# Sharing the fourth pairs' rows in three steps of two transfers, with a new order of all engines' work, in a fused attention, gMLP and channel-mix kernel

## The chip, the core and the metric

The kernel runs on one core of one Trainium2 chip. The core has TensorE (PE, with its weight loads PEld), VectorE (DVE), ScalarE (ACT), GpSimd (POOL) and SyncE (SP), each with a program of its own that it works off in order. They wait for one another by semaphores; transfers run on 16 DMA engines. The metric is the device time of one execution in microseconds (us).

## What is computed

Three blocks stand behind one another. Only `x` passes between them.

```python
# attention: B=2, H=8, S=768, D=48
for t in range(S):
    cur = einsum('bhd,bhe->bhde', u * k[t], v[t])
    y[t] = einsum('bhd,bhde->bhe', r[t], state + cur)
    state = w[t][..., None] * state + einsum('bhd,bhe->bhde', k[t], v[t])
x = y.transpose(0, 2, 1, 3).reshape(B, S, 384)
# gated MLP: d_ff = 1024, halves u and v of 512
h = gelu(x @ w_in)
v_n = layernorm(v) * g_ln
x = x + (u * (w_sg @ v_n + b_sg)) @ w_out
# channel mix
xk = mu_k * x + (1 - mu_k) * x_prev
xr = mu_r * x + (1 - mu_r) * x_prev
out = sigmoid(xr @ w_r) * (relu(xk @ w_k) ** 2 @ w_v)
```

Matrices of weights come in float64; the kernel rebuilds float32 values from their two halves.

## The kernel before

**Tiling.** Tokens are cut into four groups g = 2b + half of 384 (batch b, half of the sequence), each in three chunks of 128. The attention is computed by chunks: within one through a masked 128 by 128 matrix, between them through a state. Heads go in pairs: per group there are four *units* (unit i is pair i % 4 of group i // 4, 16 in all). Per group three *packs* of 128 rows hold the decay products. A pack's rows are 48 + 16 + 48 + 16: two heads of a pair, and in each 16-row strip a third of the fourth pair. So the fourth unit of a group (3, 7, 11, 15) reads its k and r from a gathered tile `six`, filled from the three packs by token `6` (L284 to L287), and its result must be spread again over 16-row strips of xT: that is `share` (L409 to L412).

**Order.** All instructions are laid down by a table of tokens, ORDER (L34 to L88), read from left to right; one token is one step, which may issue on any engine. Within an engine the table's order is the program's order. No scheduler changes it. The tokens that matter here, with the unit's or the pack's number behind the letter:

- per pack: `L`, `q` load the decays wt and the rows rk; `D` a scan (L258); `a`, `j`, `g` the bound, reciprocal and backward scan (L261, L265, L268); `K` and `d` products with rk (L276, L272); `6` as above.
- per unit: `V` loads vT (L301, a tile with one buffer), `w` loads vk (L305, two buffers); on PE `T` (ptr, L325), `A` (pA, L336), `P` (pa, L340), `S` (pkv, L348), `I` (py, L392), `J` (py, L398); on DVE `m` am (L366), `n` t = pa * vT (L372, the last reader of vT), `s` the state scan sc (L377), `O` the result py + t (L407); on ACT `k`, `p`, `c`, `x` copies, among them kvs (L361; a GpSimd memset of kvs is L358), wps (L353), sx (L383); `o` is `share`.
- `X` splits xT in a high and a low part (xs_hi L431, xs_lo L433); `v` is one of the generators of the first dense product, pv, of one group and chunk (L197 to L199, three products of the high and low parts), with layer statistics through GpSimd (L450 to L452: add, power, add) and ACT (L449, L454, vn_hi L459); `u` (pu), `M` (ps), `W` (po), `E` (pk), `R` (pr), `Z` (po) are the others.
- `C<i>.x` etc. are the steps that rebuild and split piece i of the weights (DVE L163, L168, L172, L178; ACT L175, L184): 0 to 11 w_in, 12 to 23 w_sg, 24 to 31 w_out, 32 to 43 w_k, 44 to 59 w_v, 60 to 65 w_r.
- `e` issues one filler product on PE, `idle`, that nobody reads.

All transfers are issued by SP, in the table's order, so a transfer whose data are not ready holds up all that follow it in SP's program.

Of the kernel before, what the change touches and what calls it, by code (L numbers as in the profile page):

```python
# [40 lines left out]
C4.x V4 s3 A4 q5 C4.b x3 L5 T4 j4 m4 C8.l p5 C6.l I3 k4 C4.t g4 C4.h S4 C4.r n4 C4.q N3 d4 f4 J3 c4 K4 A5 C4.o O3 64 s4 T5 D5 x4 63 P5 m5 k5
p6 I4 w5 a5 K5 L6 j5 C6.x J4 C5.l C8.x C6.b V6 C8.b w6 O4 e e o3 C6.t e P6 C8.t C6.h g5 C8.h S5 C8.o f5 C6.o e d5 e c5 e e e C5.x e 65 s5 T6
n6 x5 A6 C5.b V5 D6 k6 I5 X0.1.h X0.2.h m6 S6 X0.0.h J5 a6 c6 C5.t X0.0.l C5.r A7 j6 w7 n5 p7 C5.h s6 T7 C5.q V7 O5 q6 x6 P7 L7 m7 k7 C7.l I6
C6.r C5.o p8 g6 C6.q S7 J6 n7 c7 X0.1.l V8 f6 v0.0 s7 q7 w8 d6 x7 D7 T8 v0.0 O6 A8 C7.x k8 K6 v0.0 I7 a7 C7.b q8 j7 X0.2.l p9 C10.l P8 C7.t
L8 g7 C7.r J7 C7.h C7.q K7 S8 d7 f7 66 v0.2 v0.0 n8 q9 c8 O7 L11 C8.r s8 v0.0 o7 C7.o T9 x8 C10.x v0.0 P9 v0.2 m8 I8 k9 D8 v0.2 w9 A9 V9
C10.b C8.q a8 C9.l J8 K8 p10 C11.l m9 v0.1 j8 C10.t g8 C10.h v0.2 C10.o f8 S9 d8 v0.1 u0.0 L9 n9 68 v0.2 D11 v0.1 P10 67 C9.x O8 u0.0 C9.b
A10 c9 C11.x V11 C9.t T10 s9 w10 C9.h C9.r D9 u0.1 x9 C11.b k10 K9 v0.1 I9 a9 C11.t u0.1 j9 C9.o C11.h S10 g9 v0.1 J9 c10 C11.o v0.1 f9 u0.3
s10 C9.q L10 O9 C13.l p11 C10.r m10 T11 x10 C25.l P11 d9 C10.q A11 u0.3 v0.2 C11.r n11 u0.2 p12 C19.l C11.q m11 V10 C13.h w11 C25.x k11 D10 B
I10 X1.0.h X1.1.h C25.b A12 a10 X1.2.h C13.o u0.2 X1.1.l J10 C19.h X1.2.l v1.1 j10 n10 w12 m12 q10 V12 g10 C20.l S11 v1.1 O10 P12 a11 C19.o
c11 j11 v1.1 C25.t v1.2 C18.l s11 f10 g11 p13 x11 d10 T12 f11 n12 I11 K10 k12 C20.h X1.0.l S12 v1.2 C20.o P13 c12 J11 v1.2 s12 T13 v1.1 O11  # L50
69 x12 u1.3 610 v1.1 k13 v1.1 I12 p14 o11 u1.3 v1.2 v1.0 C18.h v1.2 C18.o v1.2 w13 J12 v1.0 q11 V13 A13 O12 v1.0 C12.l u1.0 w14 m13 C23.l S13
u1.0 u1.1 c13 d11 v1.0 K11 v1.0 T14 s13 611 u1.1 n13 A14 x13 v1.0 P14 m14 k14 C23.h I13 C12.h C23.o C12.o S14 C21.l V14 p15 J13 c14 A15 s14
w15 C17.l O13 T15 x14 m15 P15 C21.h k15 n14 u1.2 C21.o C14.l C17.h I14 C17.o X2.1.h u1.2 X2.1.l C24.l S15 X2.0.h V15 J14 X2.2.h X2.0.l c15
X2.2.l v2.1 C14.h O14 s15 C14.o x15 C24.x C22.l n15 v2.2 v2.1 C24.b C24.t v2.1 C24.r I15 v2.2 C28.l v2.0 C24.q v2.2 C22.h v2.1 C22.o J15
C25.r C15.l v2.0 M1.0 C26.l O15 C25.q o15 v2.0 v2.2 C15.h C15.o M1.2 M1.0 C27.l | M1.0 v2.0 C25.h C24.h C25.o C24.o C26.x C28.x C26.b u2.1
C28.b C26.t C28.t C26.h M1.2 C26.r C28.h C26.o C30.l C26.q M1.3 M1.2 u2.1 C27.x C28.o C27.b C27.t C27.h C27.r C27.o C27.q C31.l C30.x C30.b
u2.2 C28.r M1.3 C28.q C29.l C30.t M1.3 C30.h C30.o u2.3 u2.2 C31.x C31.b C31.t M0.3 u2.3 C29.x C29.b C31.h C29.t C31.o C29.h C29.r C29.o
C29.q C32.l C30.r C30.q C33.l M0.1 M0.3 C31.r M0.3 C31.q C34.l C32.x C32.b C32.t C33.x M0.0 C32.r M0.1 C32.h C35.l C32.q C33.b C32.o M0.1
C34.x C33.t C34.b C33.r C34.t C33.h C39.l M1.1 C33.q C33.o M0.0 C34.h C34.r C35.x M0.0 C34.q C40.l C34.o C35.b C35.t C39.x C35.h u2.0 C39.b
C35.r C35.o C35.q C36.l C39.t M1.1 C39.h M0.2 C40.x u2.0 M1.1 X3.1.h C40.b X3.0.h C39.o X3.2.h C40.t X3.0.l C40.h C36.x C40.o C36.b v3.0  # L60
X3.1.l v2.0 C36.t v2.2 M0.2 v2.0 C36.h v2.1 M0.2 v3.1 v3.0 v2.1 C36.r v2.2 v3.0 C37.l C36.o X3.2.l C36.q v3.2 v3.1 v3.1 v3.0 C37.x u3.1 C37.b
v3.2 C37.t C37.r u3.0 v3.2 C38.l v3.1 C37.h u3.2 v3.1 C37.o u3.0 v3.1 v3.0 u3.3 C38.x v3.2 v3.0 u3.2 C38.b v3.2 C38.t u3.3 v3.2 C38.h G0.1.h
C38.o M3.3 G0.3.h G0.1.l G0.0.h G0.3.l G0.2.h G0.0.l u3.1 G0.2.l C37.q C38.r M2.0 C38.q C41.l M3.3 C39.r M3.3 C39.q C42.l C40.r C40.q C44.l
C41.x M2.2 M2.0 C41.b M2.0 C42.x C41.t C42.b C41.r C42.t C41.h C46.l C41.q C41.o M3.0 M2.2 C42.h C42.r C44.x M2.2 C42.q C43.l C42.o C44.b
C44.t C46.x C44.h C46.b C44.o M2.1 C46.t M3.0 C46.h C46.o C43.x M3.0 C43.b C43.t C43.r W0.2 C43.h C47.l M2.1 C43.q C43.o M2.1 C44.r C44.q
C45.l M3.2 W0.2 C47.x C47.b C47.t C47.h C45.x C47.o C45.b C45.t W0.0 M3.2 C45.r C45.h C48.l M3.2 C45.q C45.o C46.r C46.q C51.l W0.1 W0.0
C47.r C47.q C50.l C48.x C48.b M3.1 W0.1 G1.2.h G1.1.h C48.t C51.x G1.0.h G1.2.l C48.h C51.b C48.r G1.1.l G1.3.h C49.l G1.0.l C48.q G1.3.l
M2.3 C51.t M3.1 C51.h C51.o M3.1 C50.x C48.o C50.b C49.x C50.t C49.b C50.h W1.0 C49.t M2.3 C49.r C49.h H0 C53.l C49.q C50.r W1.2 C50.q C52.l
# [849 lines left out]
```

## Time and profile before

| | us |
|---|---|
| median of 3 runs | 349.54 (347.97 to 351.85) |
| the profiled execution | 350.13 |
| its span | 348.3 |
| PE busy in the span | 329.8 |
| DVE busy | 257.4 |
| ACT busy | 210.0 |
| POOL busy | 45.0 |

The span is the time from the first to the last instruction of the execution that was profiled. A row of the timeline gives start, duration, engine, line and operation; in brackets stands how long the engine sat idle before it, and whose end released it ("issue" where the profile names nothing). A tile's buffer number is left out of its name. DMA rows of SP (SPq) give the time of the issue, not of the transfer.

### The profile page before, as it was taken

To read this page: it belongs to the slowest core of one execution; us is meant where nothing else is said; L and a number is where in the kernel's file an instruction comes from. 1 tells how busy PE (TensorE), PEld (TensorE's weight loads), DVE (VectorE), ACT (ScalarE), POOL (GpSimd) and SP (SyncE) were. 2 spreads that over 40 slices of the span, in tenths; PEclk is the share of its full clock that TensorE was granted. 3 is DMA by queue.
4 is the path that set the end of the run, shared out by engine and by line. 5 is a ranking of instruction groups with operands and counts; after the bars stand their busy time and mean duration, and the time that the engine had idled before them with its cause. 6 is when DMAs were issued, how large, how long until landed. Compare 5 with 4: busy or idle time off the path is not lost.

```text
span 348.3 us, 6211 instructions
## 1 busy us (share of the span) xinstructions
PE 329.8 (95%) x2162; PEld 295.0 (85%) x2165; DVE 257.4 (74%) x575; ACT 210.0 (60%) x575; POOL 45.0 (13%) x92
## 2 busy tenths in 40 slices
...
GB/s 211 186 197 249 177 98 202 204 187 92 212 69 147 147 95 60 85 145 45 46 85 84 85 81 11 25 45 73 110 1 70 0 2 68 0 2 23 45 41 34
DMA packets 22435, 32.52 MB, mean 93 GB/s; under 512 B 2944, under 2 KB 18816, under 8 KB 22400
## 3 DMA queue, kind: packets, MB, share of 16 engines
...
q8 instruction: 18, 0.29, 0.4%
...
## 4 chain that ended last, share of the span: by engine, by line
PE 70%; DVE 8%; DMA 4%; ACT 4%; POOL 1%; issue 1%; SPq 1%; DVEq 0%; ACTq 0%
PE po L557 11%; PE ps L197 5%; PE ps L199 5%; PE ps L198 5%; PE pk L199 5%; PE pk L198 5%; PE pk L197 5%; PE po L199 4%; PE po L197 4%; PE po L198 4%; DMA vT<-in_rkv_dram 3%; PE pr L199 2%; PE pr L197 2%; PE pr L198 2%; PE pu L197 2%; PE pu L198 2%
## 5 line engine op out<-in xcount | busy, mean ns | idle before, releaser
L197 PE MATMUL ps<-wsg,vn_hi 128*128 128x384 f32 x96 | 32.7, 340 | 0.0
L198 PE MATMUL ps<-wsg,vn_hi 128*128 128x384 f32 x96 | 32.5, 338 | 0.0
L199 PE MATMUL ps<-wsg,vn_lo 128*128 128x384 f32 x96 | 32.5, 338 | 0.0
L199 PE MATMUL pk<-xk_hi,wk_lo 128*128 128x384 f32 x96 | 32.4, 337 | 0.0
L198 PE MATMUL pk<-xk_lo,wk_hi 128*128 128x384 f32 x96 | 32.3, 336 | 0.0
L197 PE MATMUL pk<-xk_hi,wk_hi 128*128 128x384 f32 x96 | 32.3, 336 | 0.0
L536 ACT CAST kk_hi<-kr 128x384 fp32r<-128x384 f32 x32 | 16.0, 512 | 20.1 <-PE po L557 11.3
L529 ACT ACTIVATE kr<-pk 128x384 f32<-128x384 f32 x32 | 15.7, 490 | 18.9 <-PE pk L199 15.0
L531 DVE TENSOR_TENSOR kr<-kr 128x384 f32<-128x384 f32 x32 | 17.7, 556 | 12.7 <-ACT kr L529 12.2
L560 DVE TENSOR_TENSOR rr<-po,rr 128x384 f32<-128x384 f32 x12 | 6.7, 555 | 24.6 <-PE po L199 10.0
L557 PE MATMUL po<-pl_win_hi,kk_hi 128*128 128x384 f32 x81 | 23.0, 338 | 0.0
L538 DVE TENSOR_TENSOR kk_lo<-kr,kk_hi 128x384 fp32r<-128x384 f32 x32 | 17.5, 555 | 2.6 <-ACT kk_hi L536 2.1
L383 ACT COPY sx<-sc 48x144 f32<-48x144 f32 x32 | 14.5, 454 | 8.0 <-DVE sc L377 7.6
L450 POOL TENSOR_SCALAR ln<-ln 128x1 f32<-128x1 f32 x12 | 6.3, 524 | 94.1 <-ACT vj L449 94.1
L197 PEld LDWEIGHTS ps<-wsg,vn_hi 128*128 128x128 f32 x96 | 18.0, 188 | 0.5 <-DVE sg L476 0.3
L557 PE MATMUL po<-pl_win_lo,kk_hi 128*128 128x384 f32 x63 | 18.4, 338 | 0.0
L557 PE MATMUL po<-pl_win_hi,kk_lo 128*128 128x384 f32 x54 | 18.2, 337 | 0.0
L199 PEld LDWEIGHTS pk<-xk_hi,wk_lo 128*128 128x128 f32 x96 | 18.0, 188 | 0.0
L198 PEld LDWEIGHTS pk<-xk_lo,wk_hi 128*128 128x128 f32 x96 | 18.0, 188 | 0.0
L197 PEld LDWEIGHTS pk<-xk_hi,wk_hi 128*128 128x128 f32 x96 | 18.0, 188 | 0.0
L198 PEld LDWEIGHTS ps<-wsg,vn_hi 128*128 128x128 f32 x96 | 18.0, 188 | 0.0
L199 PEld LDWEIGHTS ps<-wsg,vn_lo 128*128 128x128 f32 x96 | 18.0, 188 | 0.0
...
## 6 DMA issues: line engine op xcount, KB each, us to landing
...
```

Source lines behind the costliest of these rows:

```text
L197: T.matmul(ps, lh, rh, start=(i == 0), stop=False)
L198: T.matmul(ps, lh, rl, start=False, stop=False)
L199: T.matmul(ps, ll, rh, start=False, stop=(i == n - 1))
L383: A.copy(u.sx[o:o + D, :, o:o + D], u.sc[o:o + D, :, 1:1 + NCB].rearrange("p e c -> p c e"))
L450: G.tensor_scalar_add(ln[:, 1:2], ln[:, 1:2], EPS * DH ** 3)
L529: A.activation(kr, ps, AF.Relu)
L531: V.tensor_mul(kr, kr, kr)
L536: A.copy(hi, kr)
L538: V.tensor_sub(lo, kr, hi.bitcast(F32))
L557: T.matmul(pv[g][s], l, wv[i][r], start=st, stop=(i == KF - 1 and l is ll))
L560: V.tensor_mul(rr[g][:, s, :], pv[g][s], rr[g][:, s, :])
```

## The change

`share` becomes three steps: each call issues the two transfers of one 128-row block j. The table has `o3.0`, `o3.1`, `o3.2` where it had `o3`, and the same for 7, 11 and 15, at places of their own. The whole table is in another order, with 37 instead of 35 tokens `e`. A tile mask2 is made in step `Q` by two small GpSimd copies. Branches for `u.i < HALVES` in `scores`, `weigh` and `inner` and a step `rest` (token `h`) are new, but HALVES is 0 and no token `h` stands in the table, so they never run. All other work is the same. Line numbers move by 2 to 28: vT's load is L303, n L391, s L396, O L433, share L437 and L438.

```diff
-ORDER = """L0 q0 e Q e L1 e q1 e V0 e C0.l e D0 w0 e e a0 p0 e j0 K0 e g0 e e e e d0 f0 e e e e L2 D1 e A0 60 T0 a1 p1 m0 P0 k0 j1 K1 g1 P1 n0 f1 e d1
+ORDER = """L0 q0 e e Q e L1 e C0.l e q1 e D0 V0 e w0 e a0 p0 e w1 j0 K0 e g0 e e e e d0 f0 e e e e L2 D1 e A0 60 C0.x T0 p1 a1 m0 P0 k0 j1 C0.b g1 e e e
...
+HALVES = 0
...
+    mask2 = keep.tile([P, 64], F32, name="mask2")
...
         def share(u):
-            for j in range(KX):
-                nc.sync.dma_start(xT[u.g][48:64, j, 1:], u.t1[16 * j:16 * j + 16, :])
-                nc.sync.dma_start(xT[u.g][112:128, j, 1:], u.t1[64 + 16 * j:64 + 16 * j + 16, :])
+            j = u.shared = getattr(u, "shared", -1) + 1
+            nc.sync.dma_start(xT[u.g][48:64, j, 1:], u.t1[16 * j:16 * j + 16, :])
+            nc.sync.dma_start(xT[u.g][112:128, j, 1:], u.t1[64 + 16 * j:64 + 16 * j + 16, :])
...
+            G.tensor_copy(mask2[:64, :], mask[:64, :64])
+            G.tensor_copy(mask2[64:, :], mask[64:, 64:])
```

SP's program around o3, before. In names of tiles the group or unit and a serial number stand behind the name: vT_0_1_1 is the vT of batch 0, half 1, pair 1, unit 5; t1_0_0_3 is the result of unit 3.

```order
L411 DMA xT0_83<-t1_0_0_3_465 16x384
L412 DMA xT0_83<-t1_0_0_3_465 16x384
L287 DMA six_147<-pk_1_2_608 16x1158 x2
L301 DMA vT_0_1_1_719<-in_rkv_dram 112x384
L305 DMA vk_0_1_3_762<-in_vt_dram 128x288
L301 DMA vT_0_1_3_775<-in_rkv_dram 112x384
```

The two rows of t1_0_0_3 on top are the last of three such pairs, which stand together. The same place after the change:

```order
L437 DMA xT0_84<-t1_0_0_3_492 16x384
L438 DMA xT0_84<-t1_0_0_3_492 16x384
L289 DMA six_148<-pk_1_2_641 16x1158 x2
L303 DMA vT_0_1_1_733<-in_rkv_dram 112x384
L437 DMA xT0_84<-t1_0_0_3_492 16x384
L438 DMA xT0_84<-t1_0_0_3_492 16x384
L307 DMA vk_0_1_3_764<-in_vt_dram 128x288
L303 DMA vT_0_1_3_787<-in_rkv_dram 112x384
```

The second pair now stands right ahead of `six`, the load of unit 5's vT comes next, and the third pair follows it; the first pair (not shown) stands eight rows before the `six` of this piece.

VectorE's program around s8 (the scan `sc_1_0_0`), before; t1_1_0_0 is n8.

```order
L276 TENSOR_TENSOR pk_2_1_842<-rk_2_1_835 128x384
L272 TENSOR_TENSOR pk_2_1_842<-pk_2_1_842,rk_2_1_835 128x2x3x128
L372 TENSOR_TENSOR t1_1_0_0_922<-pa_1_0_0_882,vT_1_0_0_820 112x384
L407 TENSOR_TENSOR t1_0_1_3_815<-py_0_1_3_869,t1_0_1_3_815 112x384
L377 SCALAR_TENSOR_TENSOR sc_1_0_0_933<-kvs0_141,wps0_143 112x240
```

And after the change:

```order
L391 TENSOR_TENSOR t1_1_0_0_929<-pa_1_0_0_865,vT_1_0_0_851 112x384
L263 TENSOR_SCALAR d1w_141<-pk_2_2_916 128x3
L433 TENSOR_TENSOR t1_0_1_3_846<-py_0_1_3_878,t1_0_1_3_846 112x384
L165 TENSOR_SCALAR winu2_0_x_950<-winu2_0_raw_853 128x256
L380 TENSOR_TENSOR am_1_0_1_952<-pA_1_0_1_933,c_sb_63 128x768
L170 SCALAR_TENSOR_TENSOR winu2_0_x_950<-winu2_0_raw_853,winu2_0_x_950 128x256
L267 RECIPROCAL d1w_141<-d1w_141 128x3
L396 SCALAR_TENSOR_TENSOR sc_1_0_0_980<-kvs0_142,wps0_144 112x240
```

Between n8 and s8 stood one product; now six rows stand there.

VectorE's program from n11 (t1_1_0_3) on, after the change; t1_1_0_2 is n10, t1_1_1_0 is n12.

```order
L391 TENSOR_TENSOR t1_1_0_3_1196<-pa_1_0_3_1174,vT_1_0_3_1082 112x384
L274 TENSOR_TENSOR pk_3_0_1128<-pk_3_0_1128,rk_3_0_927 128x2x3x128
L180 TENSOR_TENSOR wsg1_104<-wsg1_384_raw_1164,wsg1_104 128x384
L380 TENSOR_TENSOR am_1_0_3_1217<-pA_1_0_3_1189,c_sb_63 128x768
L396 SCALAR_TENSOR_TENSOR sc_1_0_3_1227<-kvs1_143,wps1_145 112x240
L391 TENSOR_TENSOR t1_1_0_2_1238<-pa_1_0_2_1102,vT_1_0_2_1201 112x384
L380 TENSOR_TENSOR am_1_1_0_1250<-pA_1_1_0_1229,c_sb_63 128x768
L433 TENSOR_TENSOR xT2_86<-py_1_0_2_1204,t1_1_0_2_1238 112x384
L260 SCALAR_TENSOR_TENSOR pk_3_1_1273<-wt_3_1_1244,d1pat_65 128x387
L391 TENSOR_TENSOR t1_1_1_0_1280<-pa_1_1_0_1254,vT_1_1_0_1252 112x384
```

Before, eight rows stood between n11 and n10 where four stand now, and n12 followed n10 at a greater distance; each of these three products reads the one buffer of vT, reloaded between.

## Rows read from the trace of the kernel before

**Rows 1.** The page, busy time of the engines
```profile
PE 329.8 (95%) x2162; PEld 295.0 (85%) x2165; DVE 257.4 (74%) x575; ACT 210.0 (60%) x575; POOL 45.0 (13%) x92
```

**Rows 2.** Busy time by stretch: length, engines, granted clock, DMA share, GB/s
```profile
40.00:60.00 20.00, 16.26 (x142) 11.43 (x139) 17.34 (x38) 11.59 (x35) 0.69 (x1) 0.91 0.60 167
60.00:80.00 20.00, 18.33 (x162) 14.16 (x160) 17.60 (x38) 15.44 (x44) 8.09 (x16) 1.00 0.60 171
80.00:100.00 20.00, 19.27 (x153) 15.04 (x150) 18.16 (x35) 17.11 (x52) 5.75 (x8) 1.00 0.54 148
...
120.00:158.00 38.00, 38.00 (x219) 36.28 (x218) 25.48 (x71) 25.51 (x78) 3.16 (x9) 1.00 0.36 98
158.00:166.00 8.00, 6.82 (x29) 4.86 (x28) 6.99 (x17) 6.85 (x18) 1.40 (x3) 1.00 0.17 58
166.00:340.00 174.00, 174.00 (x995) 173.82 (x994) 122.24 (x282) 95.24 (x247) 10.49 (x13) 1.00 0.15 44
```

**Rows 3.** Timeline of SP: the first and last share transfer, six, vT
```profile
41.77 0.52 SPq L411 DMA_DIRECT2D xT<-t  x1
...
45.22 0.71 SPq L412 DMA_DIRECT2D xT<-t  x1
46.04 1.16 SPq L287 DMA_DIRECT2D six<-pk  x2
47.30 0.52 SPq L301 DMA_DIRECT2D vT<-in_rkv_dram  x1
```

**Rows 4.** Timeline of VectorE and ScalarE, 45 to 51 us
```profile
45.06 0.55 DVE L372 TENSOR_TENSOR t<-pa,vT 112x384 f32<-112x384 f32 x1
...
50.77 0.32 ACT L353 COPY wps<-six 112x144 f32<-112x144 f32 x1 [1.33 <-DMA six<-pk]
...
51.01 0.56 DVE L372 TENSOR_TENSOR t<-pa,vT 112x384 f32<-112x384 f32 x1 [1.54 <-DMA vT<-in_rkv_dram]
```

**Rows 5.** Busy time by stretches of 2 us, columns as in rows 2
```profile
48.00:50.00 2.00, 0.66 (x6) 0.29 (x2) 0.71 (x3) 1.44 (x5) 0.00 (x0) 1.00 0.65 156
50.00:52.00 2.00, 1.22 (x14) 1.13 (x15) 0.99 (x2) 1.12 (x4) 0.00 (x0) 1.00 0.08 29
...
54.00:56.00 2.00, 2.00 (x24) 1.75 (x25) 1.63 (x4) 1.26 (x7) 0.00 (x0) 0.50 0.93 323
```

**Rows 6.** Timeline of TensorE: py, pkv, and the first pv of group 1
```profile
53.14 1.62 PE L392 MATMUL py<-pk,sx 112*112 112x128 f32 x6 [0.37 <-ACT sx L383]
...
78.43 0.91 PE L392 MATMUL py<-pk,sx 112*112 112x128 f32 x6 [1.09 <-ACT sx L383]
79.27 0.49 PE L348 MATMUL pkv<-vk,kT 128*64 128x48 f32 x11
...
88.59 0.50 PE L197 MATMUL pv<-win_hi,xs_hi 128*128 128x512 f32 x1
```

**Rows 7.** Timeline: the scans s8 and s9 and what they waited for
```profile
63.74 0.82 ACT L454 ACTIVATE v<-v,ln 128x512 f32<-128x512 f32 x1 [0.88 <-POOL ln L452]
...
64.83 0.66 DVE L377 TENSOR_TENSOR_SCAN sc<-kvs,wps 112x240 f32<-112x240 f32 x1 [1.00 <-ACT kvs L361]
...
76.55 0.30 POOL L358 MEMSET kvs<- 112x48 f32 x2
...
76.78 0.66 DVE L377 TENSOR_TENSOR_SCAN sc<-kvs,wps 112x240 f32<-112x240 f32 x1 [1.40 <-POOL kvs L358]
...
77.36 0.94 DVE L258 TENSOR_TENSOR_SCAN pk<-wt,d1pat 128x387 f32<-128x387 f32 x1
```

**Rows 8.** Timeline of TensorE at 165 us
```profile
165.04 0.50 PE L199 MATMUL pv<-win_hi,xs_lo 128*128 128x512 f32 x1 [0.90 <-DVE xs_lo L433]
```

**Rows 9.** The tile vT, its 16 loads
```profile
DMA to landing us min/median/max: 2.2/3.1/5.4
```

**Rows 10.** Groups of instructions by line: count, busy us, mean ns, idle before
```profile
L366 DVE TENSOR_TENSOR am<-pA,c_sb 128x768 f32<-128x768 f32 x16 | 15.2, 948 | 0.3 <-PE pA L336 0.3
...
L640 PE MATMUL idle<-d1pat 128*128 128x512 bf16 x32 | 10.0, 451 | 1.8 <-POOL d1pat L118 1.4 <-issue 0.3
```

More of the change, by code (lines that the diff above doesn't have):

```diff
@@ L41 @@
[L41 to L68, printed above, removed]
@@ new lines @@
+C10.b j8 v0.0 s8 k9 V9 C10.t p10 w9 g8 x8 C9.l K8 C11.l C10.h I8 f8 v0.1 v0.0 C10.o A8 d8 v0.2 u0.1 m8 v0.0 68 v0.2 D11 J8 o7.1 u0.1 v0.2 S9
+O8 u0.0 w10 c9 C9.x n9 v0.0 s9 V11 v0.0 C9.b T10 L9 C11.x x9 C9.t 67 P10 C11.b v0.0 C9.r I9 C9.h o7.2 C11.t C9.q C9.o A10 C11.h k10 D9 C10.r
+J9 u0.0 C11.o C10.q S10 K9 w11 p11 m10 u0.2 C19.l C11.r c10 O9 C11.q s10 P11 u0.2 a9 j9 x10 g9 T11 C19.h A11 n11 k11 d9 V10 f9 I10 p12 C19.o
+S11 m11 J10 c11 s11 A12 w12 n10 x11 L10 T12 m12 V12 P12 C18.l k12 O10 C21.l u0.3 D10 I11 X1.1.h n12 p13 X1.2.h S12 a10 X1.1.l V13 u0.3 J11
@@ new lines @@
+j10 X1.2.l C18.h g10 C21.h v1.2 69 X1.0.h C21.o c12 a11 X1.0.l f10 w14 s12 q10 u1.0 C18.o v1.2 O11 p14 j11 x12 o11.0 g11 v1.0 u1.0 v1.2 f11
+d10 I12 v1.0 K10 A13 v1.0 610 J12 m13 v1.2 P13 v1.2 w13 O12 C15.l u1.2 v1.2 o11.1 n13 v1.0 C20.l T13 v1.0 q11 u1.2 v1.1 v1.0 V14 C15.h C14.l
+k13 C15.o o11.2 C20.h S13 v1.1 C20.o u1.3 c13 K11 v1.1 d11 P14 u1.3 s13 611 T14 C14.h x13 C14.o A14 k14 n14 I13 v1.1 m14 V15 S14 C25.l v1.1
+J13 C23.l c14 v1.1 B P15 p15 w15 s14 C24.l O13 A15 x14 n15 T15 C25.x m15 I14 C23.h k15 C25.b C23.o u1.1 C25.t C12.l J14 X2.2.h X2.0.h X2.2.l
@@ new lines @@
+S15 u1.1 O14 v2.2 X2.1.h X2.0.l c15 C24.x X2.1.l C12.h C24.b s15 v2.1 C12.o v2.2 C24.t C22.l x15 C24.r v2.2 I15 C26.l C24.q v2.0 v2.1 C22.h
+v2.1 C22.o J15 C28.l v2.2 C25.r M1.0 O15 v2.0 C17.l o15.0 C25.q v2.0 v2.1 M1.1 C17.h M1.0 C17.o o15.1 M1.0 v2.0 C13.l M1.3 M1.1 M1.1 o15.2
+C13.h C13.o M1.2 C27.l M1.3 M1.3 | C25.h C24.h C25.o C24.o C26.x C27.x M0.1 C26.b C27.b C26.t M1.2 C26.h C26.r C26.o M1.2 C26.q C29.l C28.x
+C27.t C28.b C27.r C28.t C27.h u2.3 C30.l C27.q M0.1 C28.h C27.o C28.r M0.1 C28.q C31.l C28.o u2.1 C29.x u2.3 C29.b C29.t C29.h C30.x C29.r
@@ L89 @@
+Z2.5 E3.2 E3.2 E3.7 Z2.6 E3.7 E3.7 E3.1 Z2.7 E3.0 z2.2 E3.2 E3.7 E3.2 y2.2 E3.7 E3.1 E3.6 E3.0 E3.1 E3.0 E3.1 E3.0 E3.1 E3.3 E3.0 E3.6 E3.6
+E3.4 E3.6 E3.3 E3.6 E3.3 E3.5 E3.3 E3.4 E3.3 E3.4 R2.0 E3.5 E3.4 E3.5 E3.4 E3.5 R2.1 R2.0 E3.5 z2.0 y2.0 Z3.0 R2.1 Y3.1.1.b z2.1 Y3.1.0.b
+Y3.1.1.c y2.1 Y3.1.2.b Y3.1.0.c Y3.1.2.c R3.1 R3.2 R3.1 Z3.1 R3.2 R3.0 z3.1 y3.1 Z3.2 R3.0 z3.0 y3.0 z3.2 y3.2"""
 EPS = 1e-6
@@ L332, in scores @@
             u.pA = ps_A.tile([P, 2, 512], F32, name=f"pA_{u.n}", tag="pA")
+            if u.i < HALVES:
+                for c in range(NCB):
+                    for s, t, o2 in ((0, 0, 0), (64, 64, 0), (0, 64, 64)):
+                        for o in (0, 64):
+                            T.matmul(u.pA[s:s + 64, o // 64, c * C + o2:c * C + o2 + 64], u.kinv[o:o + D, c, s:s + 64], u.rp[o:o + D, c, t:t + 64],
+                                     start=True, stop=True)
+                return
             for c in range(NCB):
```

71 lines of the change are left out of this document (47 added, 24 removed).

## The prediction

> **What bounds the kernel now.** I read the page's first part, then the span cut at the stalls. TensorE is busy for 329.8 of 348.3 us [rows 1], and from 166 to 340 us it is busy in all 174.00 [rows 2]: nothing done off TensorE there can shorten the end. What it has left to gain is idle time before that: by subtraction in [rows 2] 3.74 us in 40 to 60, 1.67 in 60 to 80, 0.73 in 80 to 100, none from 120 to 158, 1.18 in 158 to 166. Before 40 us the engines start up, and I expect nothing there.
>
> Why does TensorE idle before 100 us, and would it run faster if VectorE did? In 40 to 100 VectorE is busy 17.34, 17.60 and 18.16 of each 20 us: it is the engine nearest to its limit, and TensorE waits for what it makes. So there a stall of VectorE moves everything behind it. It sat idle 2.66 us in 40 to 60 and 2.40 in 60 to 80, 5.06 in all. The rows name the causes:
>
> - The **share stall**. SP issues the six row transfers of o3 one behind another from 41.77 to 45.22 us, then two `six` transfers, and only at 47.30 the load of vT for unit 5 [rows 3]. That buffer was free since 45.06 + 0.55 = 45.61, when unit 6's product with vT had ended; SP came 1.69 us late. The load landed 3.7 us later, and VectorE stood 1.54 us until 51.01 [rows 4]. On the same queue `six` was late, and ScalarE idled 1.33 us for it [rows 4]. TensorE, which needs `six` for unit 7 at 50.78, lost more than the wait: it was busy 0.66 of 2 us in 48 to 50 and 1.22 in 50 to 52, and then the clock was granted at 0.50, the 1.2 GHz level, in 54 to 56 [rows 5]. Six py products took 1.62 us there, against 0.91 at 78.43 [rows 6], so the slow clock cost about 0.7 on that group alone.
> - **Scan s8** waited 1.00 us at 64.83 for kvs from ScalarE, which had itself waited 0.88 for GpSimd's part of the layer statistics (add, power, add) [rows 7].
> - **Scan s9** waited 1.40 us at 76.78 for a GpSimd memset of kvs that stood in GpSimd's order behind such a part (token order; the memset is the last row ahead of s9 in [rows 7]); TensorE waited 1.09 for what followed, at 78.43 [rows 6, 7].
> - **Late**, at 165.04, a pv product waited 0.90 us for xs_lo [rows 8].
>
> The span starts and ends 1.8 us short of the profiled execution's 350.13 us, which itself lies 0.6 over the median of 349.54. I make the sum against 350.1 and take 0.6 off.
>
> **The change, part by part.** No instruction of the dense part is added or removed; DMAs are the same in number and size. So every term is a wait that goes or comes, or work that moves across a need.
>
> *The share in three steps.* Two transfers now stand where six did; in SP's order vT for unit 5 passes ahead of the last pair, and the first pair passes ahead of `six`. VectorE's n5 stands farther behind n6: the work between (t, am, a decay scan, conversions) comes to 3.7 us by their row durations, less some 0.08 for the overlap of neighbours (76.78 + 0.66 against 77.36 in [rows 7]), against 3.04 before. A landing takes 3.1 us at the median, 2.2 to 5.4 at the ends [rows 9], and two share transfers may still be ahead of it, 1.1 us at the spacing of [rows 3] if it is held up. The 2.66 us should fall to about 0.4 (0 to 1.7). Without TensorE's idle stretch the clock should not fall; I give that no term of its own, as TensorE waits for VectorE again right behind. The same split at o7 also unblocks the queue; at o11 and o15 TensorE is already full (120 to 158, none idle), so nothing.
>
> *The two scans.* s8 now stands some 4 us of VectorE work behind the steps that feed it (d1w, am, t1, three conversions), where before it followed t1 at once; s9 gets 3.5 us instead of 2.2 behind the group's statistics. 1.00 and 1.40 become together 0.3 (0 to 1.2).
>
> *New short gaps.* vT has one buffer (bufs=1), so the load for the next unit may start only when the last product with it is done. The new order puts n10 only 2.77 us of VectorE work behind n11, and n12 2.19 behind n10; before these gaps were 3.76 and 5.42. Against a landing of 3.1 that is 0.33 + 0.91, with the issue about 1.4 us of new waiting (0 if landings are 2.2; 4.9 if they are 5.4, both plus issue). I take the median because the queue's two late cases had six transfers ahead of them.
>
> VectorE's waits thus go from 5.06 to 0.4 + 0.3 + 1.4 = 2.1: **-3.0 us**.
>
> *What stands ahead of the group-1 products.* The first pv of group 1 starts at 88.59 [rows 6], when its xs_lo comes. VectorE has more ahead of that need in the new order: C19.o, s11, n10, m12, O10, n12, j10 and one more xs_lo, less C13.o and two steps of C25, +2.9 us by row durations (am 948 ns [rows 10], s 0.66 [rows 7], products and xs_lo as the 0.55 at 45.06 [rows 4]). TensorE has more as well that it does while it waits: S11, S12, T12, P12, I11, J11 at 0.4 to 0.9 each (pkv 0.49 and py 0.91 in [rows 6]), about 3.3, and two more fillers, 0.4. So TensorE's wait at this need changes by +2.9 - 3.7 = **-0.8 us**, while the two fillers lengthen its work by **+0.4** (the `idle` line is 10.0 us for 32, at most 0.6 for two [rows 10]).
>
> *Late.* One wk piece's steps (2.8 us of VectorE) now stand behind X3.2.l instead of ahead of it, with 0.4 more TensorE work ahead: the waits of 158 to 166, 1.18 us, should be gone: **-1.2**.
>
> *Two GpSimd copies* of mask2 stand behind the blku products that others need, early, on an engine busy 13% [rows 1]: 0 (up to 0.4, at GpSimd's 0.30 us for two memsets of 48 columns in [rows 7]). C0's load goes ahead of q1 and V0, at the start: 0 to 0.3.
>
> Sum: -3.0 - 0.8 + 0.4 - 1.2 = -4.6. A wholly new order has waits that I can't see (semaphores that were never late before); I add 0.8 for them (0 to 3). That gives -3.8: 350.1 - 3.8 = 346.3, less 0.6 is **345.7 us** against the median.
>
> *A rule that speaks against it.* The Trainium skill ("DMA: Bandwidth & Descriptors", "Issuing engines are not separate DMA queues") says that all DMAs interleave on the same 16 engines and that the time to initiate one is usually small relative to the DMA itself. By that, the order of issue hardly moves vT's landing, and the gain of 2.3 on the 2.66 would be lost: 348.0. Here the trace differs: the DMA engines were busy 0.65 in 48 to 50 and 0.08 in 50 to 52 [rows 5] while the issue was 1.69 us late [rows 3, 4], so the issue itself was the delay.
>
> **The rivals.**
>
> *B, the vT wait only moves.* Landings at the short gaps take what the load at 47.30 took, 3.7, and n5 still waits: 0.9 + 1.5 at n10 and n12, 1.2 at n5, 0.5 elsewhere, so VectorE keeps about 4.4 of 5.06. Sum -0.7 - 0.8 + 0.4 - 1.2 + 0.8 = -1.5: 348.0. For it: one buffer still. Against: fewer transfers ahead.
>
> *C, another engine binds.* ScalarE is busy 17.11 of 20 in 80 to 100 [rows 2], hardly less than VectorE. If VectorE comes 3 us earlier, ScalarE may give back only half; and a TensorE that comes earlier to 158 may meet a VectorE that is no earlier (it waits for wk loads), so the -1.2 is lost as well. Sum -1.5 - 0.8 + 0.4 + 0.8 = -1.1: 348.4.
>
> *D, slower: landings near 5.* All loads still go down one SP queue, which now blocks at three share steps per group instead of one, and the reload gaps are short in more places (by the same row durations 3.69 us at unit 2, 3.67 at 5, 3.75 at 7, 2.77 at 10, 2.19 at 12). Landings of 5.0 each lie inside the range of [rows 9]; the waits are then 1.3 + 1.3 + 1.3 + 2.2 + 2.8 = 8.9, with the scans' 0.3 it is 4.1 more than the 5.06 removed. With the late gain lost as in C the sum is 4.1 - 0.8 + 0.4 + 0.8 = +4.5: 354.0. At 4.8 it is 353.1; from about 4.0 down it turns into a gain. Against it: 3.1 is the median of 16, and this needs 5 of the 15 reloads near the largest.
>
> *E, all of it.* No wait stays and none comes: -5.06 - 0.8 + 0.4 - 1.2 = -6.7, so 342.8.
>
> The change could also do nothing at the end if the removed waits were never on the path; the chain of the idle times at TensorE speaks against it (1.09 at 78.43 directly behind s9).
>
> **How the numbers follow.** My forecast 345.7 (own range 343.8 to 347.5) gets 0.50, E 0.10, B 0.15, C 0.13, D 0.12. A measurement of this kernel tells about 1% from no change, so faster means under 346.05 and slower over 353.04. Faster: E whole, six tenths of the forecast's case and a little of B and C, 0.10 + 0.30 + 0.02 = 0.42. Slower: D from landings of 4.8, 0.11. Same: the rest, 0.47. The range, 342.2 to 352.8, leaves out a part of E below and nearly all of D above, with what may go wrong beyond C.
>
> **What would show it.** In the trace of after: vT for unit 5 issued within 0.5 us of n6's end, ahead of the last share pair; VectorE's wait before n5 under 0.5; the granted clock 1.00 from 48 to 58; no wait over 0.4 before s8 and s9; waits for vT of about 0.4 and 1.0 before n10 and n12; the first pv of group 1 near 88 instead of 88.59 although 2.9 us more of VectorE lie ahead of it, with TensorE's wait before it down by some 4; TensorE idle under 0.3 in 155 to 166. Wrong if n10 and n12 wait 2 us or more each, if ScalarE is what TensorE waits for in 60 to 100, or if TensorE falls idle again behind 120 us.

## The result, and the profile after

| | before | after |
|---|---|---|
| median of 15 runs, us | 349.55 (347.33 to 351.85) | 346.13 (345.40 to 348.09) |
| profiled execution, us | 350.13 | 346.07 |
| its span, us | 348.3 | 344.3 |

The ratio is 0.9913, with a 95% interval of 0.9891 to 0.9936: 3.0 us shorter (2.2 to 3.8). The medians differ by 3.4 us and the two profiled executions by 4.06, so what is read from the two traces adds up to about 1 us more than the ratio gives. The forecast was 345.7 us, 3.8 below the median of before. The median lies 0.1 us above the 346.05 under which the prediction spoke of "faster".

The busy times after, by the page and by the stretches of [rows 2] (columns as there):

```profile
PE 326.6 (95%) x2167; PEld 293.9 (85%) x2167; DVE 257.5 (75%) x575; ACT 209.3 (61%) x575; POOL 39.7 (12%) x94
```

```profile
40.00:60.00 20.00, 17.49 (x165) 12.53 (x164) 19.03 (x39) 13.66 (x42) 1.76 (x5) 1.00 0.63 173
60.00:80.00 20.00, 18.60 (x173) 15.04 (x172) 19.40 (x40) 17.34 (x51) 7.49 (x14) 1.00 0.57 160
80.00:100.00 20.00, 18.89 (x168) 15.73 (x167) 17.09 (x32) 16.25 (x43) 3.25 (x8) 1.00 0.47 122
...
120.00:158.00 38.00, 38.00 (x221) 36.61 (x220) 25.61 (x69) 26.32 (x80) 3.17 (x9) 1.00 0.36 100
158.00:166.00 8.00, 8.00 (x42) 7.33 (x41) 6.16 (x15) 7.38 (x21) 3.83 (x8) 1.00 0.14 33
166.00:340.00 174.00, 172.92 (x986) 172.28 (x984) 120.52 (x280) 91.32 (x239) 3.65 (x8) 1.00 0.15 44
```

VectorE's idle time fell from 2.66 to 0.97 us in 40 to 60 and from 2.40 to 0.60 in 60 to 80: 3.5 of the 5.06. TensorE's own idle time fell by less: 1.23 and 0.27 us. The rest of what came back before 100 us stands in the clock column, 0.91 before and 1.00 now in 40 to 60.

To see where the gain lies I compare when TensorE begins the same kind of work. Four rows of after, then three of before (the first pv, the first ps and the last po; the first pv of group 1 is in [rows 6]):

```profile
53.67 0.70 PE L199 MATMUL pv<-win_hi,xs_hi 128*128 128x512 f32 x1
89.49 0.50 PE L199 MATMUL pv<-win_hi,xs_hi 128*128 128x512 f32 x1
124.19 0.44 PE L199 MATMUL ps<-wsg,vn_hi 128*128 128x384 f32 x1
339.16 0.34 PE L201 MATMUL po<-pl_win_hi,kk_lo 128*128 128x384 f32 x1
```

```profile
56.66 0.50 PE L197 MATMUL pv<-win_hi,xs_hi 128*128 128x512 f32 x1
126.67 0.44 PE L197 MATMUL ps<-wsg,vn_hi 128*128 128x384 f32 x1
343.17 0.34 PE L199 MATMUL po<-pl_win_hi,kk_lo 128*128 128x384 f32 x1
```

At each such place the new order has some more of TensorE's work done already: 0.4 us of fillers at all of them, and at the first pv of group 1, with them, 3.7 by the prediction's count and 3.4 by TensorE's busy time between the two first pv. With that added, after is ahead by 56.66 - 53.67 + 0.4 = 3.4 us at the first pv, by 88.59 - 89.49 plus 3.4 to 3.7 = 2.5 to 2.8 at group 1's, by 2.5 + 0.4 = 2.9 at the first ps, and by 4.0 + 0.4 = 4.4 at the last po. So **all of the gain before 126 us arises before the first pv**; half a microsecond to one is lost again up to 89 us; and 1.5 more come behind 126 us. Of these 1.5, 0.6 are idle time that went (1.18 us before, 0.58 after); the other 0.9 stand in TensorE's busy time for the same products, and why is not shown.

That the gain arises at the share stall shows in unit 7's pA, the product that needs `six`. Before (two rows), then after:

```profile
48.48 0.46 PE L336 MATMUL pA<-six 48*128 48x128 f32 x2 [0.28 <-issue]
50.78 0.90 PE L336 MATMUL pA<-six 48*128 48x128 f32 x10 [1.84 <-issue]
```

```profile
48.89 0.94 PE L346 MATMUL pA<-six 48*128 48x128 f32 x12
```

By 48.89 the new order has done one transposition (0.44 us) and one filler that the old one has still to do or lacks, so up to there the two are within about 0.3 us of each other. Nearly all of the 3 us come between there and the first pv.

The share's place after, in the views of [rows 3 to 6]:

```profile
44.40 1.14 SPq L289 DMA_DIRECT2D six<-pk  x2
46.28 0.34 SPq L303 DMA_DIRECT2D vT<-in_rkv_dram  x1
46.67 0.51 SPq L437 DMA_DIRECT2D xT<-t  x1
47.23 0.59 SPq L438 DMA_DIRECT2D xT<-t  x1
```

```profile
45.73 0.52 DVE L391 TENSOR_TENSOR t<-pa,vT 112x384 f32<-112x384 f32 x1
...
50.57 0.56 DVE L391 TENSOR_TENSOR t<-pa,vT 112x384 f32<-112x384 f32 x1 [0.44 <-DMA xT<-t]
```

```profile
48.00:50.00 2.00, 2.00 (x26) 1.41 (x22) 1.96 (x5) 1.64 (x5) 0.00 (x0) 1.00 0.31 68
50.00:52.00 2.00, 0.87 (x7) 0.71 (x6) 1.56 (x4) 2.00 (x8) 0.00 (x0) 1.00 0.13 45
...
54.00:56.00 2.00, 2.00 (x10) 1.47 (x8) 1.51 (x4) 0.96 (x3) 0.00 (x0) 1.00 1.03 361
```

vT is issued 0.03 us after unit 6's product ends (45.73 + 0.52), `six` 1.64 us earlier than before. n5 still waits 0.44 us, but by the releaser named not for vT: for the last pair of the share, whose source occupies a buffer of the tile that n5 writes (t1 has two). TensorE's idle time, 2.1 us in 48 to 52 before, is 1.1 now, and the clock holds.

What the scans and the vT loads do now (TensorE's waits for sx in 57 to 80, and the landings):

```profile
66.90 0.91 PE L411 MATMUL py<-pk,sx 112*112 112x128 f32 x6 [0.48 <-ACT sx L402]
75.04 0.91 PE L411 MATMUL py<-pk,sx 112*112 112x128 f32 x6 [0.76 <-ACT sx L402]
```

```profile
DMA to landing us min/median/max: 2.2/2.4/6.3
```

Before, TensorE waited 0.46 and 1.09 us for sx in this stretch; now 0.48 and 0.76, and 0.65 more for a pack whose rk came late. No product with vT waits for its load any more (before, n5 and one at 116.19 us, 1.39, did). VectorE waits at other places, 3.94 us in all for loads of rk and wt; before, it had one such wait, 2.01 us for rk at 107.67:

```profile
55.83 0.96 DVE L274 TENSOR_TENSOR pk<-pk,rk 128x768 f32<-128x768 f32 x1 [0.49 <-DMA rk<-in_rkp_dram]
...
87.22 0.96 DVE L260 TENSOR_TENSOR_SCAN pk<-wt,d1pat 128x387 f32<-128x387 f32 x1 [0.66 <-DMA wt<-in_wp_dram]
...
95.63 0.96 DVE L274 TENSOR_TENSOR pk<-pk,rk 128x768 f32<-128x768 f32 x1 [1.45 <-DMA rk<-in_rkp_dram]
...
105.62 0.56 DVE L278 TENSOR_TENSOR pk<-rk 128x384 f32<-128x384 f32 x1 [1.34 <-DMA rk<-in_rkp_dram]
```

### The profile page after: what moved, and what is told of

Read it like the earlier page. It is cut to its first block, busy times and chain, and to the rows that moved or that the text cites. A ratio compares the mean times of both kernels' runs of the same rounds, so it can differ in the third digit from the quotient of the medians.

```text
span 344.3 us, 6219 instructions
## 1 busy us (share of the span) xinstructions
PE 326.6 (95%) x2167; PEld 293.9 (85%) x2167; DVE 257.5 (75%) x575; ACT 209.3 (61%) x575; POOL 39.7 (12%) x94
## 4 chain that ended last, share of the span: by engine, by line
PE 63%; DVE 12%; DMA 9%; ACT 6%; POOL 5%; issue 2%; SPq 2%; DVEq 0%
PE po L583 11%; PE pk L201 5%; PE pk L200 5%; PE pk L199 5%; PE ps L199 4%; PE ps L201 4%; PE ps L200 4%; DMA rk<-in_rkp_dram 4%; PE po L201 4%; PE po L199 4%; PE po L200 4%; PE pr L199 2%; PE pr L201 2%; PE pr L200 2%; PE py L424 2%
## 5 line engine op out<-in xcount | busy, mean ns | idle before, releaser
L199 PE MATMUL pu<-xs_hi,win_hi 128*128 128x384 f32 x48 | 17.3, 361 | 0.6 <-ACT uT L493 0.6
```

The source lines that it names most:

```text
L199: T.matmul(ps, lh, rh, start=(i == 0), stop=False)
```

## The experiments

Ratios are against runs of the kernel before on the same chip; us are the ratio times 349.5.

### The share's steps in the old order: b_share3, b_share3c, b_share3d

Only o3 is split, in the kernel before; o7, o11 and o15 stay together. b_share3:

```diff
-... x4 63 P5 ... e e o3 C6.t ... V5 D6 k6 I5 X0.1.h X0.2.h m6 ... X0.0.l C5.r A7
+... x4 63 o3.0 P5 ... e e o3.1 C6.t ... V5 o3.2 D6 k6 I5 X0.1.h m6 ... X0.0.l X0.2.h C5.r A7
```

> The kernel before with only o3 split: its first pair of transfers after token 63, the second where o3 stood, the third behind unit 5's vT load (and X0.2.h two steps later, since it needs the third pair). o7, o11, o15 stay together; nothing else moves. Theory 1 (the share stall is what the change gained before 126 us): VectorE's 1.54 us before n5 falls under 0.6, the clock stays at 1.00 from 52 to 58, TensorE reaches the first product of the dense part 3 us earlier than 56.66, and the time falls by 2.3 to 3.4 us. Rival 2 (the prediction's ledger as it stood): the wait falls, but only the 2.3 us of VectorE's waits come back. Rival 3 (later waits decide): under 1 us.

Measured: 1.0066 (1.0042 to 1.0091), 2.3 us slower. n5 no longer waits for vT, but the split of xT on ScalarE is late:

```profile
50.77 0.93 ACT L431 CAST xs_hi<-xT 128x384 fp32r<-128x384 f32 x2 [3.31 <-DMA xT<-t]
```

```profile
50.00:52.00 2.00, 0.00 (x0) 0.00 (x0) 0.27 (x1) 1.24 (x5) 0.00 (x0) 1.00 0.26 74
...
56.00:58.00 2.00, 2.00 (x26) 1.73 (x24) 1.40 (x4) 1.25 (x6) 0.00 (x0) 0.50 0.96 336
```

The first split, X0.1.h, waits for all three pairs, and it must: the number in X0.1 is a chunk of 128 tokens, and the split reads that chunk in all three row blocks of xT (128x384 in the row above), while each pair fills one row block for all tokens. The expectations of this run and the next, which tie X0.2.h alone to the third pair, have this wrong. ScalarE stands there 3.31 us with kvs and the state copies behind it in its program, TensorE does nothing in 50 to 52, and the clock falls to the 1.2 GHz level for longer than before (0.50 from 54 to 60). I then moved only the third pair, and X0.2.h out of the way (b_share3c):

```diff
-... e e o3 C6.t ... V5 D6 k6 I5 X0.1.h X0.2.h m6 ... n7 c7 X0.1.l
+... e e o3.0 o3.1 C6.t ... V5 o3.2 D6 k6 I5 X0.1.h m6 ... n7 c7 X0.2.h X0.1.l
```

> The kernel before with o3's third pair alone moved, behind unit 5's vT load; the split of xT's third block, which needs that pair, goes on ScalarE from its old place to one behind kvs of unit 7, so that ScalarE does not stand behind the pair as it did with b_share3. six and vT are then issued 1.2 us earlier. Theory 1: TensorE's idle time at 48 to 51 shrinks by 1.2 us, VectorE's wait before n5 falls to 0.3 to 0.8, the first product comes 1.3 to 2 us before 56.66, time 1.2 to 2 us shorter, more if the clock stays up. Rival 2: the gain is given back behind the first product as TensorE's waits for sx grow; within 0.6 us.

Measured: 1.005 (1.0032 to 1.0069), 1.7 us slower, with the same wait, 3.67 us at X0.1.h, and the clock at 0.50 from 50 to 56. At last all the splits behind x6, as the changed kernel has them (b_share3d):

```diff
-... V5 D6 k6 I5 X0.1.h X0.2.h m6 S6 X0.0.h J5 a6 c6 C5.t X0.0.l C5.r ... O5 q6 x6 P7
+... V5 o3.2 D6 k6 I5 m6 S6 J5 a6 c6 C5.t C5.r ... O5 q6 x6 X0.0.h X0.1.h X0.2.h X0.0.l P7
```

> The kernel before with o3's third pair behind unit 5's vT load, and all three splits of xT0 (X0.0.h, X0.1.h, X0.2.h, X0.0.l) behind x6, as the changed kernel has them, since the first split waits for all three pairs. Theory 1 (what the share's steps bring hangs on where their reader stands): ScalarE's waits of 3.3 to 3.7 us in b_share3 and b_share3c go, TensorE's idle time at 48 to 51 shrinks by 1 us or more, the first product comes 1 to 3 us before 56.66, time 1 to 3 us shorter. Rival 2: the six transfers themselves, not their order against readers, set the stall; within 0.6 us of the kernel before.

Measured: 1.0024 (0.9991 to 1.0057): no difference. ScalarE's wait is gone. n5 starts 0.34 us earlier than before (50.67 for 51.01), about where it starts after the change (50.57), and VectorE stands idle 2.12 us ahead of it, since the split's xs_lo, which stood there, was moved off:

```profile
50.67 0.56 DVE L372 TENSOR_TENSOR t<-pa,vT 112x384 f32<-112x384 f32 x1 [2.12 <-DMA vk<-in_vt_dram]
```

(The releaser named is a neighbour in the queue; n5 reads vT and writes a buffer of the tile that the share reads.) But here too the clock falls, behind TensorE's waits of 1.37 us for n5 and 0.80 for the keys on ScalarE:

```profile
54.00:56.00 2.00, 1.50 (x21) 1.50 (x23) 2.00 (x4) 1.81 (x9) 0.00 (x0) 0.56 0.96 349
56.00:58.00 2.00, 2.00 (x11) 1.41 (x8) 2.00 (x4) 1.22 (x4) 0.00 (x0) 0.59 0.29 89
```

The first pv comes at 56.58, 5.9 us behind n5, where it comes 3.1 us behind it after the change. So the split brings nothing in the old order, in three placements; all three have the slow clock, and none was run with TensorE's gap filled, so what the split would bring at full clock stays open.

### The share joined again in the new order: a_join and a_join_fill

```diff
-... e o3.1 f5 ... I5 o3.2 c6 ... (o3.0 ahead of x4)
+... e o3.0 o3.1 o3.2 f5 ... I5 c6 ...
```

> The changed kernel with o3's three steps put together again, at the place of the second (ahead of the six transfers of pack 5 and of unit 5's vT). Theory 1: the share stall comes back with its idle time on TensorE and most of what the change gained before 126 us is lost, 2 to 3.4 us slower than the changed kernel. Rival: the new order put enough work between n6 and n5 (3.7 us) to hide a late vT; within 0.7 us of the changed kernel.

Measured: 0.9971 (0.9947 to 0.9995) against before, so 1.0 us of the change's 3.0 are left; the loss is 2.0 us. TensorE waits for `six` and then for n5, and the clock falls:

```profile
50.12 0.48 PE L327 MATMUL ptr<-c_sb,six 112*128 112x112 f32 x3 [1.88 <-DMA six<-pk]
...
52.69 1.59 PE L411 MATMUL py<-pk,sx 112*112 112x128 f32 x6 [1.22 <-DVE t L391]
...
57.15 1.20 PE L199 MATMUL pv<-win_hi,xs_hi 128*128 128x512 f32 x1
```

n5 is late here through `six` (issued at 46.28, after the change at 44.40), not through vT: ScalarE stands for `six`, VectorE for ScalarE, and n5 follows at 51.99 without a wait of its own (vT is issued later too, at 47.54, but no wait is put down to it).

```profile
50.06 0.32 ACT L363 COPY wps<-six 112x144 f32<-112x144 f32 x1 [3.13 <-DMA six<-pk]
...
51.65 0.43 DVE L180 TENSOR_TENSOR win_lo<-winv_x,win_hi 128x256 fp32r<-128x256 f32 x1 [2.22 <-ACT win_hi L177]
```

The clock behind it:

```profile
52.00:54.00 2.00, 1.31 (x6) 1.30 (x6) 2.00 (x5) 2.00 (x7) 0.00 (x0) 0.50 0.18 41
54.00:56.00 2.00, 2.00 (x26) 1.73 (x24) 1.28 (x3) 1.87 (x8) 0.00 (x0) 0.50 0.81 229
```

Then the same with eight fillers in TensorE's gap (a_join_fill: `j6 T7` becomes `j6 e e e e e e e e T7`).

> The changed kernel with o3's three steps together again (a_join) and eight fillers on TensorE ahead of unit 7's transposition, where it idled 1.88 us. It parts what a_join lost into waiting and slow clock. Theory 1: the clock stays at 1.00 from 50 to 60 and 1.2 to 1.8 us of a_join's loss come back, the rest is the wait itself. Rival: the loss is all wait; within 0.4 us of a_join.

Measured: 0.993 (0.9903 to 0.9957): 1.4 us of the 2.0 come back, though `six` and n5 are as late as in a_join (unit 7's transposition at 50.10, n5 at 51.97). The clock is 1.00 throughout, and the first pv comes 2.1 us earlier:

```profile
52.00:54.00 2.00, 1.33 (x22) 1.23 (x24) 2.00 (x5) 2.00 (x7) 0.00 (x0) 1.00 0.21 48
54.00:56.00 2.00, 2.00 (x18) 1.46 (x14) 2.00 (x5) 1.94 (x8) 0.00 (x0) 1.00 0.79 235
```

```profile
55.06 0.69 PE L199 MATMUL pv<-win_hi,xs_hi 128*128 128x512 f32 x1
```

So about two thirds of what the share's place costs is slow clock, one third waiting; at the first pv (53.67 after the change) it is 2.1 of 3.5 us. The two intervals overlap a little at their ends, so the parts are rough.

### The clock in the old order: b_fill

`C5.r A7` becomes `C5.r e e e e e e e e A7`; nothing else.

> The kernel before with eight more filler products on TensorE in front of unit 7's pA, where it idles at 48.5 to 50.8; all waits for vT and six stay. Theory 1 (the clock at 1.2 GHz behind that idle time is a cost of its own): the clock stays at 1.00 in 52 to 58, six py products behind it take 0.9 us instead of 1.62, and the time falls by 1.0 to 1.6 us. Rival (the prediction, which gave the clock no term because TensorE waits for VectorE again right behind): the clock stays up and the time stays within 0.4 us. If the clock falls all the same, neither is told.

Measured: 0.9954 (0.9932 to 0.9975), 1.6 us faster (0.9 to 2.4), with all transfers in their old order (unit 5's vT issued at 47.42, before at 47.30):

```profile
48.62 1.67 PE L640 MATMUL idle<-d1pat 128*128 128x512 bf16 x7 [0.16 <-issue]
...
52.85 0.91 PE L392 MATMUL py<-pk,sx 112*112 112x128 f32 x6 [0.45 <-ACT sx L383]
```

The six py products take 0.91 us where they took 1.62 [rows 6]. They start 0.3 us earlier than before, as n5 waits 1.13 us in this trace and not 1.54; the rest of the 1.8 us by which the first pv comes earlier (54.83) lies behind them, in the clock. Work that nobody reads is worth 1.6 us here. The runs of the kernel before that were taken beside the experiments point the same way: the ten with a mean granted clock of 0.998 or more average 348.5 us, the 27 with 0.990 or less 350.2.

The Trainium skill ("TensorE: Matmul & The Clock Gate", "Why this matters for your kernels") advises against idle gaps of some length between bursts of products, since the clock drops behind them. The trace agrees in kind (0.50 in 54 to 56 behind the gap [rows 5], 1.00 with the gap filled); the gap here, 1.84 us ahead of pA, is shorter than those the page names.

### The scans: b_scan and a_scan

b_scan, in the kernel before, gives each scan 2 us of other VectorE work ahead of it:

```diff
-C8.r s8 v0.0 o7 C7.o T9 x8 C10.x v0.0 P9 v0.2 m8 I8 ... T10 s9 w10 C9.h C9.r D9 u0.1 x9 C11.b k10
+C8.r v0.0 o7 C7.o T9 C10.x v0.0 P9 v0.2 m8 s8 x8 I8 ... T10 w10 C9.h C9.r D9 u0.1 C11.b s9 x9 k10
```

> The kernel before with scan s8 and its spread x8 moved behind am of unit 8, and s9 with x9 moved behind the pack scan D9 and a conversion step, so that VectorE does 2 to 2.5 us of other work while kvs comes. Prediction's step: both waits (1.00 and 1.40) nearly go, and 1.5 to 2.1 us of the time with them. Rival (TensorE's delay between 57 and 80 us is set by the chain statistics, GpSimd, ScalarE, scan, not by VectorE's load): the waits go and the time stays within 0.6 us.

Measured: 1.0125 (1.0092 to 1.0157), 4.4 us slower: neither theory's number. s8's wait is gone, s9 still waits 1.09 us for GpSimd's kvs (at 80.96). TensorE waits for the spread that comes behind the later scan, and the clock falls behind that wait:

```profile
69.16 1.20 PE L392 MATMUL py<-pk,sx 112*112 112x128 f32 x4 [2.79 <-ACT sx L383]
```

```profile
70.00:72.00 2.00, 2.00 (x16) 1.75 (x15) 0.00 (x0) 1.15 (x5) 1.07 (x3) 0.50 0.89 279
```

The 4.4 us thus hold a stretch of slow clock as well (0.60 in 68 to 70, 0.50 from 70 to 74, 0.69 in 74 to 76); the two were not parted.

a_scan goes the other way in the changed kernel: s8 back to where it stood before the change.

```diff
-... v0.2 O7 P9 ... j8 v0.0 s8 k9
+... v0.2 O7 s8 P9 ... j8 v0.0 k9
```

> The changed kernel with scan s8 moved ahead again, to right behind O7, as it stood before the change. Prediction's step: VectorE waits for kvs again, 0.5 to 1.0 us, and the time rises by as much. Rival (the spacing is worth nothing, since TensorE's waits for sx were the same 2 us in 57 to 80 in both kernels): within 0.4 us of the changed kernel, or faster as sx comes earlier.

Measured: 0.9865 (0.9824 to 0.9906) against 0.9913: not slower; perhaps faster, which the intervals don't settle. (The waits for sx, which the expectation calls the same 2 us, were 1.55 us before and 1.24 after.) VectorE does not wait for kvs there (no bracket), and the scan, and with it py, come earlier:

```profile
63.12 0.65 DVE L396 TENSOR_TENSOR_SCAN sc<-kvs,wps 112x240 f32<-112x240 f32 x1
```

```profile
65.84 0.82 PE L411 MATMUL py<-pk,sx 112*112 112x128 f32 x6
```

In the changed kernel that scan starts at 65.05 and the py at 66.90; 0.4 us of the difference were there before n8. So it is not the spacing that took s8's wait away: ScalarE copies kvs 2.2 us earlier after the change (n8 itself comes only 0.2 us earlier), since in the new order the copy stands behind no step that waits for GpSimd, as it did before for 0.88 us [rows 7]. Before, then after:

```profile
64.46 0.26 ACT L361 COPY kvs<-pkv 112x144 f32<-112x144 f32 x1
```

```profile
62.27 0.27 ACT L371 COPY kvs<-pkv 112x144 f32<-112x144 f32 x1
```

The scan is a link of the chain kvs, scan, sx, py; in b_scan, work put ahead of it delayed TensorE. What the spacing of s9 does alone was not run.

### The late splits: b_late and b_fill_late

```diff
-X3.0.l C40.h ... v3.0 X3.1.l v2.0 ... C36.o X3.2.l C36.q
+X3.0.l X3.1.l X3.2.l C40.h ... v3.0 v2.0 ... C36.o C36.q
```

> The kernel before with the last two splits of group 3 (X3.1.l, X3.2.l) on VectorE right behind X3.0.l, ahead of the steps of one w_k piece. Prediction's step: TensorE's waits of 0.28 and 0.90 us at 160 and 165 go and the time falls by 1.2 us. Rival: TensorE is full from there on only because it waited, and another wait (layer statistics, w_k pieces) takes their place; within 0.4 us.

Measured: 0.9993 (0.996 to 1.0027). In the trace the wait of 0.90 at 165 is gone, and a new one of 0.81 stands behind it:

```profile
169.94 0.44 PE L196 MATMUL pu<-xs_hi,win_hi 128*128 128x384 f32 x1 [0.81 <-ACT uT L466]
```

TensorE's idle time from 158 to 180 us is 0.98 us with the splits moved and 1.18 before.

> Both of the kernel before: eight fillers ahead of unit 7's pA, and the two late splits moved. If the two gains are independent their sum, 2.5 to 2.9 us below the kernel before, 346.7 to 347.1: within 1 us of the changed kernel, with no transfer moved. If the late waits only absorb what comes earlier, no better than b_fill.

Measured: 0.9975 (0.9955 to 0.9995), no better than b_fill: 0.9 us faster than before (0.2 to 1.6). As these are the fillers of b_fill with one edit more, the 1.6 us of b_fill may be at the high end. The interval of b_late still allows a gain of 1.4 us, so what the late splits alone are worth stays open; 1.2 is not shown.

### Loads ahead of blocked loads: a_loads and a_best

The waits for rk and wt after the change are all of one kind: on SP such a load stands behind a transfer that has to wait. In three cases that is a load that waits for its buffer, in the fourth (rk of pack 11) o11's first pair, whose data come late.

```diff
-n5 e m7 X0.0.h V7 I6 X0.2.h q6 O5 ... A12 w12 n10 x11 L10 T12 ... X1.1.l V13 u0.3 ... s12 q10 u1.0 ... x12 o11.0 ... v1.0 q11 u1.2
+n5 e q6 m7 X0.0.h V7 I6 X0.2.h O5 ... A12 L10 w12 n10 x11 T12 ... X1.1.l q10 V13 u0.3 ... s12 u1.0 ... x12 q11 o11.0 ... v1.0 u1.2
```

> The changed kernel with four loads put ahead of a load in SP's order that waits for a buffer: rk of pack 6 ahead of unit 7's vT, wt of pack 10 ahead of vk of unit 12, rk of pack 10 ahead of unit 13's vT, rk of pack 11 ahead of o11's first pair. Theory (the new order's own waits for rk and wt cost time): VectorE's waits of 0.49, 0.66, 1.45 and 1.34 us go, TensorE's of 0.65 at 56.8, 0.49 at 96.6 and 0.82 at 106.2 with them, 0.8 to 1.9 us faster than the changed kernel. Rival: they are beside the path, within 0.4 us.

Measured: 0.985 (0.9817 to 0.9882), median 343.66 us: 5.2 us faster than before, 2.2 faster than the changed kernel. All four waits of VectorE are gone (the same instructions follow their neighbours without a bracket), TensorE's three, 1.96 us, are down to one of 0.31, and the first ps starts at 121.77 instead of 124.19:

```profile
121.77 0.44 PE L199 MATMUL ps<-wsg,vn_hi 128*128 128x384 f32 x1
```

With s8 moved as in a_scan besides (a_best):

> The changed kernel with both edits that gained on it: the four loads of a_loads, and scan s8 right behind O7 as in a_scan. If the two are independent: 0.5 to 0.9 us below a_loads, 342.8 to 343.2. If the wait that the loads removed had hidden the scan's: the time of a_loads, 343.3 to 344.1.

Measured: 0.9853 (0.9825 to 0.988), the time of a_loads. The two are the fastest found; a_loads needs the fewer edits.

## Why the forecast was right, and which of its terms were not

The time lies 0.4 us from the forecast, but the sum came out by terms that were off in both directions: that it came so close is luck. The share stall, the one term whose mechanism held, was worth more than its 2.3 us by the trace; two terms (scans and group 1, -2.9 together) brought nothing that shows, and the cost of the short gaps (+1.4) did not come.

| step of the prediction | forecast, us | what the runs show |
|---|---|---|
| share, vT and `six` earlier | -2.3 | -3.4 at the first pv in the trace; 2.0 (a_join) by the times |
| the clock | no term of its own | 1.4 (a_join_fill, part of the 2.0 above), 1.6 (b_fill) |
| scans s8, s9 | -2.1 | no gain that shows; spacing brings s8 nothing (a_scan), and both scans later cost 4.4, slow clock included (b_scan) |
| new short vT gaps | +1.4 | 0: no wait for vT |
| work ahead of group 1's pv | -0.8 | void: TensorE did not wait there |
| late splits | -1.2 | -1.5 in the trace from first ps to last po, of it 0.6 idle time; nothing certain alone (b_late) |
| unseen waits | +0.8 | 2.2 by what a_loads wins back |

**Share.** The mechanism was right: the issue, not the transfer, was late. The step that failed is the size, and its reason is one sentence: "I give that no term of its own, as TensorE waits for VectorE again right behind". It does not wait long enough to hide a clock at half rate: with the gap filled and `six` and n5 as late as ever, the first pv came 2.1 us earlier and the end 1.4 (a_join_fill). The 2.66 us that the sum gave to vT were not all vT's: 1.54 were, 0.76 were xs_lo's wait for the split of xT on ScalarE (at 48.82 us), which had waited for the last share transfer, and 0.37 a scan's wait for kvs (at 55.93). And in the new order it is `six` that makes a joined share late, not vT (a_join). I also overlooked that the last pair holds a buffer of the tile that n5 writes (0.44 us), and that every split of xT reads all three blocks and so stands behind all pairs. What else of the new table the split needs to pay is not parted: b_share3d has the readers of xT behind the last pair, as the new table has, and gains nothing, with the slow clock still in it.

**Scans.** The step "1.00 and 1.40 become together 0.3" came true for VectorE (for s8 because kvs came earlier, not by the work in between), and brought no time that shows. Between the first pv of group 0 and of group 1 after lost 0.6 to 0.9 us against before. I had read VectorE as the engine that paces everything from 40 to 100, because it is the busiest. Rows of VectorE's idle time are a cost only where its program is what TensorE waits for; here TensorE's two largest waits in 60 to 80 were for sx, the end of a chain through ScalarE, GpSimd and one scan. b_scan shows the price of the wrong reading.

**Short vT gaps.** The row of landings was taken from a queue with share transfers and weight loads in it; in the new order the median is 2.4 us, not 3.1, and the gaps did not bind. They were 3.0 us each in the trace, not 2.8 and 2.2; ahead of n12 VectorE had its 0.66 us wait for wt in between. With that wait gone, n12 waits 0.17 us for vT in a_best. (The upper bound of 4.9 for this term is 5.8 by the prediction's own gaps.) Rivals B and D rested on this row too.

**Group 1.** "When its xs_lo comes" was never in a row: neither 88.59 nor 89.49 has a wait in front of it. I inferred it from a running total.

**Late and unseen.** The wait at 165 is gone; one of 0.58 for uT at 167.31 took part of its place, as one of 0.81 did in b_late. The allowance of 0.8 for waits not seen was the right sign and too small, and their kind could have been read off the order: loads of rk and wt behind transfers that have to wait.

**The signs.** Those for the share came true: vT 0.03 us behind n6, n5's wait 0.44, the clock 1.00 from 48 to 58. So did those for s8 and s9 (no wait) and for 155 to 166 us (TensorE never idle). The waits ahead of n10 and n12 and the first pv near 88 did not come. Of the signs of being wrong two came in part: in 60 to 100 ScalarE is the named releaser of 1.56 us of TensorE's waits (0.48 and 0.76 for sx, 0.32 for the keys), VectorE of 0.95, as rival C would have it; and TensorE is idle once more behind 120 us, for the 0.58.
